# Attention with a band, then an ELU layer: tiles 8 to 17 made in pairs with 512-column products, their second products deferred

## The chip, the cores and the metric

One core of one Trainium2 chip (trn2). TensorE (PE) multiplies matrices into the eight PSUM banks; VectorE (DVE) and ScalarE (ACT) work elementwise and empty the banks; GpSimd (POOL) and SyncE (SP) mostly issue transfers. The metric is device time in microseconds of one execution, median of several runs. The profile is of one execution, and its times count from the first instruction.

## The reference, cut to what matters

```python
# q, k, v: (8, 8, 576, 64) f32
mask = abs(pos[:, None] - pos[None, :]) <= 32
scores = where(mask, q @ k.T / 8, -1e9)
attn = exp(scores - max(scores)); attn /= sum(attn)
x = (attn @ v) -> (4608, 512)        # heads side by side
h = x @ w_in                          # (4608, 2048)
g = where(h > 0, h, exp(min(h, 0)) - 1)
out = g @ w_out                       # (4608, 512), f32
```

## The kernel before

**Tiles and steps.** The 4608 rows are 18 tiles of 256 rows (NT). A tile goes through 8 steps; a step makes 2 of the 16 blocks of 128 columns of h ("first products", `products`, L716): per block four matmuls of 256 columns over the four parts of x (`xT`, 128 rows each) into one half of a PSUM bank. There are 144 steps, numbered kk, in the list `order` (L684): tiles 0 and 1 interleaved, then one tile after the other. The banks h0 and h1 take turns, so step kk needs the bank of step kk-2.

**The elementwise part.** After a step's products ScalarE makes the exponential `e_sb` (L738) and VectorE subtracts one, `m_sb` (L750; on ScalarE at L748 in steps 1, 3 and 4). One step later VectorE makes `g_sb` (L761): min of m_sb and max(h, 0), which is ELU and reads the bank a last time.

**Second products.** `mm2` (L793) multiplies the g of step kk-2 (LAG = 2) with w_out: four matmuls of 512 columns (L773), two for each half of the tile, summed in the banks y0 and y1 over the tile's 8 steps. At the tile's last step ScalarE evicts one bank, VectorE the other (`y_sb`, L290 and L292) and SyncE stores both (L811). For the last tile the second half is summed as two pieces of 256 columns (L830 to L840).

**Attention** works on pairs of blocks of 64 queries: 36 pairs, two for each tile. `begin` (L617) is the step at which a pair's work starts; from pair 10 on, both pairs of tile t begin at step 8t - 14, with exceptions in the dictionary. At begin + 0 come both pairs' scores (L384, weights from kT), at + 1 and + 2 the masks `pm` on VectorE (L404), at + 2 the products with V (L416), at + 3 and + 4 the normalisations (`rc` L425, `x_st` L428, VectorE) and a DMA transpose of x_st into xT, issued on SyncE (L455). The exponentials `pu` are on ScalarE (L395).

**Inputs.** For each of the 8 batches SyncE loads q and k in four DMAs of 576 KB (L132), ScalarE (early on also VectorE) casts them in six parts (L290, L292), ScalarE writes the rows to DRAM (L319) and SyncE reads them back transposed into qT and kT (L324). The steps of loads (l_qk), V loads (l_v) and casts (from c0) are a table by batch (L642). V comes in through GpSimd's queue (L151) into `V_e`; a copy shifted by 64 rows, `V_o`, is made by four VectorE copies (L175), or for batches 2 and 3 by two DMAs on SyncE (L183).

**Order.** The schedule is by hand: `at(kk, slot, fn)` puts work into slots of step kk, and the loop at L814 issues, for each step: g of the step before, slot "dve", the first products, slot "mid", the second products, slot "end". Each engine and each DMA queue takes its instructions in this order.

Of the kernel before, what the change touches and what calls it, by code (L numbers as in the profile page):

```python
# [21 lines left out]
def kernel(  # L22
# [99 lines left out]

    def load_qk(b, which, part, engs=(nc.sync, nc.sync)):
        z, nj = part
        mj = max(nj, HJ)
        t = lpool.tile([128, 2, mj * D], FP32, tag=f"f{which}{mj}",
                       name=f"f{which}", bufs=2 if part is WHOLE else 1)
        qk_f[b, which, z] = t
        src = (q, k)[which][b, :, z:z + NC * nj, :].rearrange(
            "(g h) (c j) d -> c g h (j d)", h=2, j=nj)  # L130
        for h in range(2):
            engs[h].dma_start(out=t[:, h, 0:nj * D], in_=src[:, :, h, :])  # L132
# [161 lines left out]
    def cast_qk(b, which, part, j0, n, eng, hs=slice(0, 2)):  # L294
        z, nj = part
        if (b, which, z) not in qk_b:
            qk_b[b, which, z] = lpool.tile(
                [128, max(nj, HJ), 2 * D], BF16,
                tag=f"b{which}{max(nj, HJ)}", name="qkb",
                bufs=2 if part is WHOLE else 1)  # L300
        t = qk_b[b, which, z]
        copy_on(eng,
                t[:, j0:j0 + n, :].rearrange("p j (h d) -> p h j d",
                                             h=2)[:, hs],
                qk_f[b, which, z][:, hs, j0 * D:(j0 + n) * D].rearrange(
                    "p h (j d) -> p h j d", d=D))
# [134 lines left out]

    xT = {}

    def xT_of(i):
        t, z = i // 2, i % 2
        if z == 0:
            xT[t] = xpool.tile([128, 2, NDO, 128], BF16, tag="xT", name="xT")
        return xT[t][:, z, :, :]

    def x_evac(i, eng=nc.vector):  # L450
# [113 lines left out]
    def at(kk, slot, fn, *args):  # L564
        tasks.setdefault((kk, slot), []).append((fn, args))
# [48 lines left out]


    FIRST_TWO, FIRST_DMA, BACK_AT = 6, 10, 18
    begin = {4: 9, 5: 12, 6: 18, 8: 26, 10: 31, 12: 37}  # L617
    for i in range(FIRST_TWO, NPAIR):
        begin[i] = begin.get(i - i % 2, STEPS * (i // 2) - 14)
    for i in range(4, NPAIR):  # L620
        two = i >= FIRST_TWO
        kk, z = begin[i], i % 2 if two else 0
# [15 lines left out]
    for b in range(2, B):  # L638
        k0 = begin[first_pair(b)]


        l_qk, l_v, c0 = {2: (0, 0, 0), 3: (15, 24, 22), 4: (35, 36, 41),  # L642
                         5: (52, 52, 57), 6: (68, 68, 73),
                         7: (84, 84, 89)}[b]
        if b >= 3:
            at(l_qk, "end", load_qk, b, 0, WHOLE)
            at(l_qk, "end", load_qk, b, 1, WHOLE)
# [1 line left out]
                at(l_v, "dve", hold_v, b)  # L649
            for m in range(VS):  # L650
                at(l_v + m, "mid", load_v, b, m)
        if b <= 3:

            if b == 2:
                at(k0, "dve", rotate_v, b, 0, 1)
            at((21, 28)[b - 2], "mid", rotate_v_dma, b, 3 - b)
        else:
            for n, back in enumerate((10, 8, 3, 2)):
                m0 = 2 * (n // 2)
                at(k0 - back, "dve", rotate_v, b, m0, m0 + 2, (n % 2,))  # L660
# [12 lines left out]
        for n, (which, j0) in enumerate(  # L673
# [3 lines left out]
            if j0 == 12:  # L677
# [3 lines left out]

    order = [(z, n + m) for n in range(0, HALF, 2) for z in range(2)  # L684
             for m in range(2)]
    order += [(z, n) for n in range(HALF, STEPS) for z in range(2)]
    order += [(t, n) for t in range(2, NT) for n in range(STEPS)]
    psH, e_t, m_t, g_t, psY = {}, {}, {}, {}, {}

    def mm1(kk):  # L690
        t, s = order[kk]
        if kk == BY_PAIRS[1]:
            return
        ks = BY_PAIRS if kk == BY_PAIRS[0] else (kk,)
        tags = ((f"h{kk % 2}", "s") if kk == NSTEP - 1 else
                ("s",) if kk == 2 else ("u",) if kk == 3 else (f"h{kk % 2}",))
        for k in ks:
            psH[k] = []
        for z, tag in enumerate(tags):
            for k in ks:  # L700
                psH[k].append(ps_tile([128, FG // len(tags), TT], FP32,
                                      tag if k == kk else "u", "ps"))
        for p in range(len(ks)):
            for k in ks:
                for z in range(len(tags)):
                    products(k, z, p if len(ks) > 1 else None)
                if p == len(ks) - 1:
                    for z in range(len(tags)):
                        exponents(k, z)
                        if k == NSTEP - 1:  # L710
                            elu(k, z)


    BY_PAIRS = (2, 3)
# [1 line left out]
    def products(kk, z, pair):  # L716
        t, s = order[kk]
        ps = psH[kk][z]
        w = ps.shape[1]
        for j in range(w):  # L720
            fo = s * FG + z * w + j
            for do in range(NDO):
# [11 lines left out]
    def exponents(kk, z):  # L734
# [5 lines left out]
        if kk > 0:  # L740
            subtract(kk, z)

    def subtract(kk, z):
        e_sb = e_t.pop((kk, z))
        m_sb = mpool.tile([128, e_sb.shape[1], TT], BF16, tag="m_sb",
                          name="m_sb")
        if kk in (1, 3, 4):
            nc.scalar.activation(m_sb, e_sb, AX.Copy, bias=-1.0)  # L748
        else:
            nc.vector.tensor_scalar(m_sb, e_sb, -1.0, None, ALU.add)  # L750
        m_t[kk, z] = m_sb

    def elu(kk, z=0):
        if z == 0:
            g_t[kk] = mpool.tile([128, FG, TT], BF16, tag="g_sb", name="g_sb",
                                   bufs=6)
        if kk == 0:
            subtract(kk, z)
        ps = psH[kk][z]
# [4 lines left out]

    out_t = out.rearrange("(t ts p) c -> t p ts c", p=128, ts=TT // 128)

    def sums_to(kk, ts, j, c):
        t, s = order[kk]
        to, cs = psY[t][ts], slice(0, D_MODEL)
        if c is not None:  # L770
            cs = slice(c * D_MODEL // 2, (c + 1) * D_MODEL // 2)
            to = psY[t][ts + c][:, 0:D_MODEL // 2]
        nc.tensor.matmul(  # L773
            to,
            lhsT=g_t[kk][:, j, ts * 128:(ts + 1) * 128],
            rhs=w_out_sb[:, s * FG + j, cs],
            start=(s == 0 and j == 0),
            stop=(s == STEPS - 1 and j == FG - 1))

    def rows_out(ts, c, eng):  # L780
        t = NT - 1
        if c is None:
            src, cs = psY[t][ts], slice(0, D_MODEL)
        else:
            cs = slice(c * D_MODEL // 2, (c + 1) * D_MODEL // 2)
            src = psY[t][ts + c][:, 0:D_MODEL // 2]
        y_sb = opool.tile([128, D_MODEL], FP32,
                          tag=f"y_sb{int(eng is nc.vector)}", name="y_sb")
        copy_on(eng, y_sb[:, cs], src)
        (nc.scalar if c == 1 else nc.sync).dma_start(  # L790
            out_t[t, :, ts, cs], y_sb[:, cs])

    def mm2(kk, parts=((0, 0), (0, 1), (1, 0), (1, 1))):  # L793
        t, s = order[kk]
        if s == 0:
            psY[t] = [ps_tile([128, D_MODEL], FP32, g, "psY")
                      for g in (("h2", "t0") if t == 1 else ("y0", "y1"))]
            if t == NT - 1:
                psY[t].append(ps_tile([128, D_MODEL], FP32, "u", "psY"))
        last = t == NT - 1  # L800
        for ts, j in parts:

            for c in ((0, 1) if last and ts else (None,)):
                sums_to(kk, ts, j, c)
        if s == STEPS - 1 and not last:
            for ts in range(2):
                eng = (nc.scalar, nc.vector)[ts]
                y_sb = opool.tile([128, D_MODEL], FP32, tag=f"y_sb{ts}",
                                  name="y_sb")
                copy_on(eng, y_sb, psY[t][ts])  # L810
                nc.sync.dma_start(out_t[t, :, ts, :], y_sb)  # L811

    LAG = 2
    for kk in range(NSTEP + LAG):  # L814
        run(kk, "first")
        for n in {1: (), 2: (0, 1)}.get(kk, (kk - 1,) if kk < NSTEP else ()):
            if n >= 0:
                elu(n)
        run(kk, "dve")
        if kk < NSTEP:  # L820
            mm1(kk)
        run(kk, "mid")

        for n in {2: (), 3: (), 4: (), 5: (0, 1), 6: (2, 3), 7: (4,), 8: (5, 6)}.get(
                kk, (kk - LAG,) if kk >= LAG else ()):

            if n < NSTEP - 2:
                run(kk, n)
                mm2(n)
            elif n == NSTEP - 1:  # L830
                for part in ((n - 1, 0, 0, None), (n - 1, 0, 1, None),
                             (n - 1, 1, 0, 0), (n - 1, 1, 0, 1),
                             (n, 0, 0, None), (n, 0, 1, None)):
                    sums_to(*part)
                rows_out(0, None, nc.scalar)
                for c in range(2):
                    for part in ((n - 1, 1, 1, c), (n, 1, 0, c),
                                 (n, 1, 1, c)):
                        sums_to(*part)
                    rows_out(1, c, (nc.vector, nc.scalar)[c])  # L840
        run(kk, "end")


# [28 lines left out]
```

## Time and profile before

| | us |
|---|---|
| median of 3 runs | 303.45 (303.1 to 303.76) |
| the profiled execution, its own time | 303.12 |
| its span, first to last instruction | 301.4 |
| PE busy | 294.1 |
| DVE busy | 240.9 |
| ACT busy | 170.1 |
| POOL busy | 50.3 |
| L728, first products, x1168 | 149.2 |
| L773, second products, x592 | 147.5 |
| L761, g_sb, x145 | 99.3 |
| L750, m_sb, x142 | 61.5 |

Busy times of one engine may overlap: a matmul's end is modelled and reaches into the next one, so PE's rows add up to more than they take; the distances between starts tell the pace. A row of a timeline has start, length, engine, line, operation, what it writes and reads, and how many were merged; a bracket at its end is the engine's idle time before it and what ended that.

### The profile page before, as it was taken

The numbers are of one execution on the slowest core, as the hardware profiler recorded it, in microseconds if no ns is written. First come the engines' busy times: TensorE is split into PE (matmuls) and PEld (weight loads), VectorE is DVE, ScalarE is ACT, GpSimd is POOL, SyncE is SP. The second block draws the span as 40 slices with busy tenths as digits, with TensorE's granted clock in tenths as the row PEclk, the third lists the DMA queues.
The fourth block names the chain that finished last, engine by engine and source line by source line (L and its number), as shares of the span: only waits on it lengthen the run. The fifth ranks groups of instructions, "written<-read, shape, count | busy, mean of one in ns | idle before, by whom it ended". The sixth has DMA issues, their size and how long they took to land.

```text
span 301.4 us, 7717 instructions
## 1 busy us (share of the span) xinstructions
PE 294.1 (98%) x3118; PEld 198.4 (66%) x3118; DVE 240.9 (80%) x479; ACT 170.1 (56%) x258; POOL 50.3 (17%) x72
## 2 busy tenths in 40 slices
PE   7999999999999999999999999999999999999994
PEld 3675667677666666666666666666666666666673
DVE  6778587988787988888888888877888787877663
ACT  3783558688655567456745674466535353533332
POOL 8857103620005000410032003200000000000000
PEclk9999999999999999999999999999999999999999
DMA  9999999999967948999899979997921111111012
GB/s 190 183 200 206 187 238 366 362 147 219 254 156 191 250 111 265 234 274 143 161 258 331 157 206 256 306 148 148 270 40 72 35 72 38 70 37 70 2 70 71
DMA packets 93157, 52.68 MB, mean 175 GB/s; under 512 B 77122, under 2 KB 83010, under 8 KB 93122
## 3 DMA queue, kind: packets, MB, share of 16 engines
q1 hardware_dynamic: 47330, 35.48, 44.3%
q0 software_dynamic: 43920, 10.10, 44.2%
q10 hardware_dynamic: 1872, 6.62, 6.4%
q8 instruction: 24, 0.39, 0.6%
q14 instruction: 11, 0.09, 0.1%
HBM read 36.70 MB, written 15.34 MB: 173 GB/s over the span
## 4 chain that ended last, share of the span: by engine, by line
PE 93%; DVE 2%; ACT 1%; DMA 1%; issue 1%; DVEq 0%; ACTq 0%
PE ps L728 42%; PE psY L773 41%; PE psS L416 4%; PE psS L384 3%; DMA f<-in_q_dram 1%; PE ptx L340 1%; PE psXT L438 1%; ACT pu L395 1%; PE ptx L335 1%; DVE qkb L292 1%; PE psS L364 1%; DVE x_st L428 0%; ACT qT L290 0%; PE ps_idle L479 0%; DVE pm L404 0%
## 5 line engine op out<-in xcount | busy, mean ns | idle before, releaser
L738 ACT ACTIVATE e_sb<-ps 128x512 f32<-128x512 f32 (+1 forms) x145 | 86.2, 595 | 114.9 <-PE ps L728 106.9
L728 PE MATMUL ps<-xT,w_in_sb 128*128 128x256 bf16 (+1 forms) x1168 | 149.2, 271 | 0.0
L773 PE MATMUL psY<-w_out_sb,g_sb 128*128 128x512 bf16 (+1 forms) x592 | 147.5, 374 | 0.0
L728 PEld LDWEIGHTS <-w_in_sb 128*128 128x128 bf16 x1168 | 110.8, 98 | 36.3 <-issue 0.5
L761 DVE SCALAR_TENSOR_TENSOR g_sb<-ps,m_sb 128x512 bf16<-128x512 f32 (+1 forms) x145 | 99.3, 686 | 13.1 <-DVE m_sb L750 0.5
L750 DVE TENSOR_SCALAR m_sb<-e_sb 128x512 bf16<-128x512 f32 (+1 forms) x142 | 61.5, 433 | 34.4 <-ACT e_sb L738 32.4
L773 PEld LDWEIGHTS <-g_sb 128*128 128x128 bf16 x592 | 56.1, 98 | 38.5 <-DVE g_sb L761 0.3
L151 POOL DMA_DIRECT2D Ve<-in_v_dram x37 | 31.7, 868 | 133.5 <-PE psS L416 79.9
L395 ACT ACTIVATE pu<-psS 128x1024 bf16<-128x1024 f32 x36 | 36.5, 1021 | 1.3 <-PE psS L384 1.3
L428 DVE TENSOR_TENSOR x_st<-psS,rc 128x512 bf16<-128x512 f32 x36 | 24.9, 691 | 1.2
L290 ACT CAST qkb<-f 128x768 bf16<-128x768 f32 (+1 forms) x29 | 25.0, 861 | 0.0
L404 DVE TENSOR_TENSOR pm<-pu,masks 128x1024 bf16<-128x1024 bf16 x32 | 21.8, 682 | 0.4 <-ACT pu L395 0.4
L416 PEld LDWEIGHTS <-pm 128*64 128x64 bf16 x512 | 9.7, 110 | 7.4 <-DVE pm L404 6.1
L292 DVE COPY y_sb<-psY 128x512 f32<-128x512 f32 (+1 forms) x18 | 12.1, 670 | 1.1 <-PE psY L773 1.1
L384 PEld LDWEIGHTS <-kT 64*128 64x128 bf16 x560 | 9.3, 95 | 4.4 <-issue 4.0
L290 ACT COPY y_sb<-psY 128x512 f32<-128x512 f32 (+1 forms) x19 | 10.9, 572 | 1.7 <-PE psY L773 1.7
L416 PE MATMUL psS<-Ve,pm 128*64 128x65 bf16 x288 | 11.6, 196 | 0.1
L384 PE MATMUL psS<-qT,kT 64*128 64x64 bf16 x560 | 11.5, 191 | 0.1
L416 PE MATMUL psS<-Vo,pm 128*64 128x65 bf16 x224 | 10.3, 196 | 0.0
L175 DVE COPY Vo<-Ve 64x1040 bf16<-64x1040 bf16 (+1 forms) x22 | 9.1, 414 | 0.7
L290 ACT COPY qT<-ptx 128x1152 bf16<-128x1152 bf16 (+4 forms) x9 | 7.7, 881 | 3.4 <-PE ptx L340 2.5
L425 DVE RECIPROCAL rc<-psS 128x8 f32<-128x8 f32 x36 | 7.2, 199 | 0.9 <-PE psS L416 0.9
(54 smaller groups left out, 88.2 us busy)
## 6 DMA issues: line engine op xcount, KB each, us to landing
out_dram<-y_sb SPq DMA_DIRECT2D x35, 256.0 KB, 3.3
f<-in_q_dram SPq DMA_DIRECT2D x12, 576.0 KB, 6.3
f<-in_k_dram SPq DMA_DIRECT2D x12, 576.0 KB, 8.3
in_dram<-qkb ACTq DMA_DIRECT2D x10, 576.0 KB, 4.3
Ve<-in_v_dram POOLq DMA_DIRECT2D x21, 128.0 KB, 12.6
w_in_sb<-in_moe_w_in_dram POOLq DMA_DIRECT2D x3, 512.0 KB, 10.1
w_out_sb<-in_moe_w_out_dram POOLq DMA_DIRECT2D x3, 512.0 KB, 10.9
Ve<-in_v_dram POOLq DMA_DIRECT2D x14, 96.0 KB, 11.5
```

The source lines that it names most:

```text
L151: nc.gpsimd.dma_start(out=V_e[b % 3][p0:p1, m, :, 0:D], in_=v[b, :, lo + p0:lo + p1, :].rearrange("h p d -> p h d"))
L290: nc.scalar.copy(d_, s_)
L384: nc.tensor.matmul(psS[:, h % 2, hp * 128 + z * QB:hp * 128 + (z + 1) * QB], lhsT=keys, rhs=qT[b % 2][base:base + 64, hp, QB * qb:QB * (qb ...
L395: nc.scalar.activation(pu, _bap(psS, [psS.ap[0], [1, 1024]]), AX.Exp, scale=SCALE)
L404: nc.vector.tensor_mul(pm, pu, _bap(mm, [mm.ap[0], [0, H], [1, 2 * QB]]))
L416: nc.tensor.matmul(psS[QB * z:QB * (z + 1), par, hp * VD:(hp + 1) * VD], lhsT=pm[:, par * HP + hp, z * QB:(z + 1) * QB], rhs=vv[:, qb // 2 ...
L428: nc.vector.tensor_mul(x_st, _bap(psS, [psS.ap[0], [VD, HP], [512, 2], [1, D]]), _bap(rc, [rc.ap[0], [2, HP], [1, 2], [0, D]]))
L728: nc.tensor.matmul(o, lhsT=w_in_sb[:, do, fo * 128:(fo + 1) * 128], rhs=r, start=(do == 0), stop=(do == NDO - 1))
L738: nc.scalar.activation(e_sb, ps, AX.Exp)
L750: nc.vector.tensor_scalar(m_sb, e_sb, -1.0, None, ALU.add)
L761: nc.vector.scalar_tensor_tensor(g_t[kk][:, z * w:(z + 1) * w, :], ps, 0.0, m_t.pop((kk, z)), ALU.max, ALU.min)
L773: nc.tensor.matmul(to, lhsT=g_t[kk][:, j, ts * 128:(ts + 1) * 128], rhs=w_out_sb[:, s * FG + j, cs], start=(s == 0 and j == 0), stop=(s == ...
```

## The change

- From tile 8 on (WIDE) two tiles share a step: one block of h for 512 rows, four matmuls of 512 columns instead of eight of 256. The xT of two tiles is one buffer; the operand is four runs of 128 columns. Steps, exponentials, m_sb and g_sb keep their number and size.
- Second products of tiles 2 to 16 come from a list `todo`, in the old order, up to four in a step; in "light" steps (begin + 0, 5, 6, from pair 16 on also 7) three, until 48 are behind. By the code's counting 12 are behind at step 18, 36 at step 64, 48 from step 87 on. An eviction follows its tile's last sum, and no further sum is issued in that step. g_sb gets 23 buffers instead of 6.
- The last tile's second products all come after everything else, as pieces of 512, 384 and 128 columns; VectorE evicts the last two, and ScalarE's queue stores the last.
- Attention begins earlier: at 8t - 18 instead of 8t - 14 from tile 10 on (tiles 7, 8 and 9 at 42, 47, 53 instead of 42, 50, 58), and loads, V loads and casts of batches 4 to 7 with it by 4 or 5 steps.
- At begin + 4 of tiles 5 to 9 the subtraction is on ScalarE. V_o of batch 4 is made by DMA instead of by VectorE.
- The load and cast buffers of half and whole batches share two slots.

```diff
-        mj = max(nj, HJ)
-        t = lpool.tile([128, 2, mj * D], FP32, tag=f"f{which}{mj}",
-                       name=f"f{which}", bufs=2 if part is WHOLE else 1)
+        t = lpool.tile([128, 2, SJ * D], FP32, tag=f"f{which}",
+                       name=f"f{which}")
...
+    WIDE = 8
     def xT_of(i):
-        t, z = i // 2, i % 2
+        n = 2 if i < 2 * WIDE else 4
+        t, z = i // n * n // 2, i % n
         if z == 0:
-            xT[t] = xpool.tile([128, 2, NDO, 128], BF16, tag="xT", name="xT")
+            xT[t] = xpool.tile([128, n, NDO, 128], BF16, tag=f"xT{n}",
+                               name="xT", bufs=4 if n == 2 else 2)
...
-    begin = {4: 9, 5: 12, 6: 18, 8: 26, 10: 31, 12: 37}
+    begin = {4: 9, 5: 12, 6: 18, 8: 26, 10: 31, 12: 37, 14: 42, 16: 47, 18: 53}
     for i in range(FIRST_TWO, NPAIR):
-        begin[i] = begin.get(i - i % 2, STEPS * (i // 2) - 14)
+        begin[i] = begin.get(i - i % 2, STEPS * (i // 2) - 18)
...
-        l_qk, l_v, c0 = {2: (0, 0, 0), 3: (15, 24, 22), 4: (35, 36, 41),
-                         5: (52, 52, 57), 6: (68, 68, 73),
-                         7: (84, 84, 89)}[b]
+        l_qk, l_v, c0 = {2: (0, 0, 0), 3: (15, 24, 22), 4: (30, 31, 36),
+                         5: (48, 48, 53), 6: (64, 64, 69),
+                         7: (80, 80, 85)}[b]
...
-        if b <= 3:
+        if b <= 4:
...
-            at((21, 28)[b - 2], "mid", rotate_v_dma, b, 3 - b)
+            at((21, 28, 40)[b - 2], "mid", rotate_v_dma, b, int(b == 2))
...
-    order += [(t, n) for t in range(2, NT) for n in range(STEPS)]
+    order += [(t, n) for t in range(2, WIDE) for n in range(STEPS)]
+    made = {(t, n * FG + j): (kk, j * TT)
+            for kk, (t, n) in enumerate(order) for j in range(FG)}
+    for t in range(WIDE, NT, 2):
+        for fo in range(NFO):
+            for z in range(2):
+                made[t + z, fo] = len(order), z * TT
+            order.append((t, fo))
...
+        if t >= WIDE:
+            for do in range(NDO):
+                nc.tensor.matmul(
+                    _bap(ps, [ps.ap[0], [128, 4], [1, 128]]),
+                    lhsT=w_in_sb[:, do, s * 128:(s + 1) * 128],
+                    rhs=xT[t][:, :, do, :],
+                    start=(do == 0), stop=(do == NDO - 1))
+            return
...
+    on_scalar = {1, 3, 4} | {begin[2 * t] + 4 for t in range(5, 10)}
...
-                                   bufs=6)
+                                   bufs=23)
...
+    todo = [(t, n * FG + j, ts) for t in range(2, NT - 1)
+            for n in range(STEPS) for ts in range(2) for j in range(FG)]
+    light = {begin[i] + n for i in range(FIRST_TWO, NPAIR)
+             for n in ((0, 5, 6) if i < 16 else (0, 5, 6, 7))}
+    LEAD = 10 * 2 * FG
+    def more_sums(kk):
+        behind = (kk + 1 - STEPS * 2) * 2 * FG - (576 - 64 - 32 - len(todo))
+        n = 3 if kk in light and behind < LEAD + 8 else 4
+        while todo and n:
+            t, fo, ts = todo[0]
+            if made[t, fo][0] > kk - LAG:
+                break
+            todo.pop(0)
+            if fo == 0 and ts == 0:
+                begin_sums(t)
+            sums_to(t, fo, ts)
+            n -= 1
+            if fo == NFO - 1 and ts == 1:
+                for ts in range(2):
+                    rows_out(t, ts)
+                break
+    def last_sums():
+        t = NT - 1
+        begin_sums(t)
+        for ts, c, eng, queue in ((0, 0, nc.scalar, nc.sync),
+                                  (1, 1, nc.vector, nc.sync),
+                                  (1, 2, nc.vector, nc.scalar)):
+            for fo in range(NFO):
+                sums_to(t, fo, ts, c)
+            rows_out(t, ts, c, eng, queue)
...
-    for kk in range(NSTEP + LAG):
+    kk = 0
+    while kk <= NSTEP or todo:
...
+        if kk >= 2 * STEPS + LAG:
+            more_sums(kk)
...
+        kk += 1
+    last_sums()
```

## The prediction

> **What bounds the kernel now.** I read the busy table of the page, then the chain of work that ended last, then the timelines of TensorE, VectorE and SyncE in a stretch with attention.
>
> ```profile
> PE 294.1 (98%) x3118; PEld 198.4 (66%) x3118; DVE 240.9 (80%) x479; ACT 170.1 (56%) x258; POOL 50.3 (17%) x72
> ...
> PE 93%; DVE 2%; ACT 1%; DMA 1%; issue 1%; DVEq 0%; ACTq 0%
> ```
>
> TensorE is busy nearly throughout and carries 93% of the chain. A busy PE may still be a slow one, so the starts decide (timeline of PE; start, length, count):
>
> ```profile
> 218.35 1.04 PE L728 MATMUL ps<-xT,w_in_sb 128*128 128x256 bf16 x8
> 219.23 1.03 PE L773 MATMUL psY<-w_out_sb,g_sb 128*128 128x512 bf16 x4
> 220.09 1.04 PE L728 MATMUL ps<-xT,w_in_sb 128*128 128x256 bf16 x8
> 220.96 1.03 PE L773 MATMUL psY<-w_out_sb,g_sb 128*128 128x512 bf16 x4
> ```
>
> Step 102 starts at 218.35, step 103 at 220.09: 1.737 us. Eight first products take 0.873 (109 ns each, start to start), four second products 0.864 (216 each), with nothing between: the matrix engine is at its pace. From 20 us on all starts together exceed that pace by about 9 us, some 8 of them at the changes of shape round the attention's small products. Under 1 us is waiting, so no wait worth removing is left; what remains to gain is instruction count and the end.
>
> How near is the next limit? The bank that a step's products fill is free when VectorE has made the g_sb of two steps before (timeline of DVE, same stretch):
>
> ```profile
> 218.85 0.69 DVE L761 SCALAR_TENSOR_TENSOR g_sb<-ps,m_sb 128x512 bf16<-128x512 f32 x1
> 219.46 0.20 DVE L425 RECIPROCAL rc<-psS 128x8 f32<-128x8 f32 x1
> 219.69 0.69 DVE L428 TENSOR_TENSOR x_st<-psS,rc 128x512 bf16<-128x512 f32 x1
> 220.30 0.42 DVE L750 TENSOR_SCALAR m_sb<-e_sb 128x512 bf16<-128x512 f32 x1
> 220.82 0.69 DVE L761 SCALAR_TENSOR_TENSOR g_sb<-ps,m_sb 128x512 bf16<-128x512 f32 x1
> ```
>
> The last row is the g_sb of step 102. It ends at 221.51, and step 104, which needs its bank, starts at 221.83: 0.32 spare, of which 0.05 is the signal (at 206.50 PE started 0.054 after the g_sb that it had waited for). Where nothing queues on VectorE the spare is 0.55 (step 103, for one); after a normalisation, as here, 0.32.
>
> **The change part by part.**
>
> *Half as many first products in tiles 8 to 17.* 640 products of 256 columns become 320 of 512, on the path throughout. Two of the old take 218 ns and one of 512 columns takes 216 in the rows above: 320 x 2.2 ns = 0.7 us gained. The weight loads that go (98 ns each) lay under the products. VectorE's and ScalarE's counts per step stay.
>
> The Trainium skill (TensorE: Matmul & The Clock Gate, Back-to-back issue gap) gives 131 ns for a sustained product of 512 columns; by that this part would gain 320 x 87 ns = 28 us. The rows have 216 for the same product, so the measurement decides.
>
> *The end.* Now the last product ends at 297.60, the last store lands at 300.45, the span closes 0.93 later. Afterwards the last piece is 128 columns on VectorE (684 ns for 512 and 425 for 256 make some 295) instead of 256 on ScalarE (372), and the 256 KB and 192 KB pieces leave earlier: 0.06 + 0.30 + 0.03 + 2.25 (the 128 KB store's landing) = 2.64 after the product instead of 2.85. I take 0.2 gained (0 to 0.45). The products of the last tile cost the same in sum (16 x 216, 16 x 162, 16 x 56).
>
> *The backlog.* Paired tiles need all 16 blocks before the first of the two can be summed, so the second products must be deferred: in "light" steps three are issued, not four, until 48 lie behind (step 87). PE's total is unchanged; each light step is 216 ns shorter while VectorE's and ScalarE's work in it stays. Two light steps in a row eat 0.43 of the 0.55 spare: no wait by themselves. With anything else on VectorE there is one, and everything on PE behind it waits too. Counting forward from the starts above: the V rotations (0.43 each, at steps 67, 68, 76, 83, 84, all light) cost 0.19, 0.20, 0.14, 0.20, 0.20; step 81 evicts a tile and step 82 normalises, ahead of light step 83: 0.39. Together 1.3 us. In steps 18 to 63 the same sum gives 0.2 at step 25 (a cast of 0.85 us behind two light steps), 0.3 at 37 and 0.2 at 60 to 62; there five subtractions go to ScalarE, so I take 0.4 of this 0.7.
>
> *The eviction of psY moves.* Before, it came at step 105, beside a long attention step. The order of the built program now has it at steps 90, 98, 106, 114 and 122, just where the normalisation delays VectorE, between subtraction and g_sb. Its price, from the place where it stands now:
>
> ```profile
> 225.26 0.43 DVE L750 TENSOR_SCALAR m_sb<-e_sb 128x512 bf16<-128x512 f32 x1 [0.33 <-ACT e_sb L738]
> 225.61 0.68 DVE L292 COPY y_sb<-psY 128x512 f32<-128x512 f32 x1
> 226.21 0.68 DVE L761 SCALAR_TENSOR_TENSOR g_sb<-ps,m_sb 128x512 bf16<-128x512 f32 x1
> ```
>
> Subtraction to g_sb is 0.95 instead of 0.52: 0.43 later. Against 0.32 - 0.05 of spare, and 0.02 that the shorter steps take: 0.19 of waiting, five times: 0.9 us. The chain of VectorE thus gives 1.3 + 0.4 + 0.9 = 2.6 us (0 if every spare is larger than I read, 3.5 with the early 0.7 and casts of ScalarE in the way).
>
> *Loads pulled forward on SyncE.* Attention starts four steps earlier, and q/k loads with it. In two places this turns the queue's order round: the four loads of batch 4 (issued at step 30) now stand ahead of the k transpose of batch 3 (step 32), those of batch 5 (48) ahead of that of batch 4 (49). Before, the transpose went first (SyncE's timeline):
>
> ```profile
> 121.01 2.72 SPq L324 DMA_TRANSPOSE kT<-in_dram  x1
> 123.77 1.24 SPq L132 DMA_DIRECT2D f<-in_q_dram  x2
> 125.05 1.60 SPq L132 DMA_DIRECT2D f<-in_k_dram  x2
> 126.71 3.17 SPq L455 DMA_TRANSPOSE xT<-x_st  x2
> ```
>
> The transposes of xT behind these loads show what that place costs; the summary of xT has
>
> ```profile
> DMA to landing us min/median/max: 2.4/2.7/9.7
> ```
>
> and the two here landed after 9.0 and 8.6, after the last load (134.06, 10.3 after the first was issued). The k transpose (0.59 MB, about 3.5 us of transfer, 5.8 from issue to landing alone) would land some 13.8 after the first load's issue. Batch 3: the loads can start at 79.5, as soon as SyncE is through with the q transpose, so kT is there at 93.3; the scores that need it come at 92.0 (before: 93.9; nine deferred products earlier): 1.3 late at most, nothing if the transpose does not queue; I take 0.5. Batch 4: loads 5.0 after the start of step 45, kT at +18.8, its scores at +15.5 (eight steps, now 14.7, and one set of products): 3.3 late at most, 0 at least; the xT rows are the nearest, but they had V loads beside them from the start, so I take 1.9. Behind the waiting weight load stands all of PE.
>
> The Trainium skill (DMA: Bandwidth & Descriptors, Queues, rings and completion order) says that SyncE's transfers share one row of rings, taken in order on each DMA engine, which speaks against this order; by it both waits would come whole, 4.6 us, and without it none. The skill's page TensorE: Matmul & The Clock Gate (Part 1: The HAM clock gate) puts the engine to half clock after some 3.4 us without work, which such a wait comes near; no row here shows it, the granted clock being 9 tenths or more in every slice.
>
> *Off the path.* Four V copies (0.43 each) of batch 4 leave VectorE for two DMAs on SyncE, under attention's lead; shared load buffers are reused only after casts of two batches back, long done. If one were not, SyncE would stop at the load, and its later transposes with it.
>
> **Sum** on the profiled execution (303.12, 301.4 of it span): -0.7 - 0.2 + 2.6 + 2.4 = +4.1, so 307.2; the median of the runs shown is 0.33 higher: **307.5**.
>
> **The rivals.**
> - *The transposes come in time* (0.21). For it: before, k landed 4 to 8 us ahead of its scores in the later batches. Against: the 9.0 us rows. VectorE's waits stay: 303.45 - 0.9 + 2.6 = 305.2 (304 to 306).
> - *The spare holds* (0.25, the other side). Before, PE waited under 1 us in 280 with VectorE at 80%; if the five subtractions on ScalarE and the long steps between the light ones absorb the eviction and rotations, and k lands early, only the gain is left: 302.5 (302 to 302.8). It decides as soon as all waits together stay under 0.3 us; at 0.9 nothing is left.
> - *Gain and waits cancel* (0.10): waits of 0.3 to 1.5 us, 302.85 to 304.05.
> - *Worse than forecast* (0.05): every wait at its upper end, -0.9 + 3.5 + 4.6 = +7.2, 310.6.
> - The forecast itself, both kinds of waiting: 0.39, 305.6 to 309.8.
>
> A measurement of this kernel tells some 0.2% (0.6 us) from no change: faster 0.25, same 0.10, slower 0.65. The range of 8 in 10 runs from 302.3, inside the clean case, to 309.8.
>
> **What would show it.** Products of 512 columns starting every 216 ns; half as many weight loads for the first products of tiles 8 to 17; PE waiting for g_sb by 0.2 at steps 92, 100, 108, 116, 124 and by 0.1 to 0.4 in 67 to 86; weight loads of the scores idle on the transposes of kT at steps 37 and 53, by 0.5 and 2 us. I am wrong if PE shows no wait there, or if a product that reads four runs of 128 columns streams slower than 216 ns (each 10 ns more is 3.2 us).

## The result, and the profile after

The changed kernel takes 327.07 us (median of 6 runs, 325.02 to 329.94), the kernel before, run beside it, 303.55 (303.1 to 303.78): ratio 1.076, 95% interval 1.071 to 1.081. Here and below a ratio leaves out slow runs, those more than 1.5% above the fastest of their kernel (one of these six, two of four in e7_v_later). The prediction said 307.5 with a range of 302.3 to 309.8: the direction was right, the time lies 17 us above the range. The profiled execution took 327.38, its span is 325.5, 24.1 more than before.

The page of the changed kernel (span; busy time by engine; granted clock by slice; the chain that ended last, by engine):

```profile
span 325.5 us, 7073 instructions
...
PE 301.8 (93%) x2798; PEld 168.8 (52%) x2798; DVE 237.1 (73%) x469; ACT 172.9 (53%) x261; POOL 50.0 (15%) x72
...
PEclk9999999999995999859999999999999999999999
...
PE 65%; DMA 15%; DVE 8%; ACT 4%; issue 3%; SPq 2%; POOL 1%; ACTq 0%; DVEq 0%; POOLq 0%
```

TensorE's share of the chain fell from 93% to 65%, and DMA, 1% before, now carries 15% (the chain follows a late transfer back to its issue, so this share is larger than the time waited). Two slices show a granted clock of half; before, none did. VectorE is less busy than before and is not the new bound. The view of waits names the transfer (engine, line, releaser: us in total, times, longest):

```profile
PEld L381 <- DMA kT<-in_dram: 14.0, 2, 7.5
PE psS L381 <- DMA kT<-in_dram: 13.6, 2, 7.4
...
PE psY L798 <- ACT y_sb L289: 1.4, 2, 0.9
```

Two waits of the scores for the k transpose make 13.6 us. TensorE's timeline round the first (start, length, operation, count, idle before and releaser):

```profile
93.62 0.52 PE L381 MATMUL psS<-qT,kT 64*128 64x64 bf16 x24
101.54 0.40 PE L381 MATMUL psS<-qT,kT 64*128 64x64 bf16 x8 [7.39 <-DMA kT<-in_dram]
...
103.12 1.92 PE L745 MATMUL ps<-xT,w_in_sb 128*128 128x256 bf16 x8
```

24 of the 32 score products use what is there; the other 8 wait 7.39 us for the k transpose of batch 3. Then, at 103.12, eight first products take 1.92 us; with the clock full they take 1.04 in this view. The table by stretches (engine, us busy and instructions, then granted clock, DMA share, GB/s) shows why:

```profile
101.70:105.00 3.30, 3.30 (x20) 1.86 (x17) 0.00 (x0) 0.00 (x0) 0.00 (x0) 0.50 1.17 267
105.00:115.00 10.00, 10.00 (x125) 6.73 (x123) 7.21 (x14) 7.50 (x11) 0.00 (x0) 1.00 0.33 94
...
140.70:146.00 5.30, 5.30 (x28) 2.83 (x23) 3.03 (x6) 2.90 (x4) 0.00 (x0) 0.50 0.47 128
```

After each of the two waits TensorE runs on at a granted clock of 0.50, until 105.06 and until 146.02. Step 38 took 2.69 us instead of the 1.74 of a step of its kind, and the whole costs about 4.5 us (half of the 3.30 and of the 5.30 in these stretches, and some 0.3 in the scores just ahead of the second). SyncE's timeline shows the transfer itself:

```profile
79.64 1.67 SPq L131 DMA_DIRECT2D f<-in_q_dram  x2
81.35 1.30 SPq L131 DMA_DIRECT2D f<-in_k_dram  x2
87.16 7.72 SPq L321 DMA_TRANSPOSE kT<-in_dram  x1
94.97 1.22 SPq L457 DMA_TRANSPOSE xT<-x_st  x1
```

The k transpose was issued at 87.16, and issuing it alone held SyncE for 7.72 us (2.72 in the line shown of before). It landed at 101.49, 14.3 after its issue; the one of batch 4, issued at 126.18, landed at 139.84, 13.7 after. In the kernel before the same two took 5.8 and 5.4. The summary of the k transposes, before and after, and what GpSimd's queue moved beside the first one (V, from 84 to 102 us: packets, MB, share of the 16 DMA engines):

```profile
DMA to landing us min/median/max: 4.6/5.8/6.8
```

```profile
DMA to landing us min/median/max: 4.0/7.1/14.3
```

```profile
q0 software_dynamic: 4688, 0.59, 58.1%
```

The shared products are as fast as forecast (TensorE's timeline, steps 100 and 101):

```profile
231.68 1.04 PE L731 MATMUL ps<-xT,w_in_sb 128*128 128x512 bf16 x4
232.55 1.03 PE L798 MATMUL psY<-w_out_sb,g_sb 128*128 128x512 bf16 x4
233.41 1.03 PE L731 MATMUL ps<-xT,w_in_sb 128*128 128x512 bf16 x4
```

233.41 - 231.68 = 1.73 for a dense step (1.727 over many) against 1.737: 0.8 us gained over 80 steps. The eviction stands where the forecast put it (VectorE's timeline, steps 98 and 99):

```profile
230.01 0.41 DVE L769 TENSOR_SCALAR m_sb<-e_sb 128x512 bf16<-128x512 f32 x1
230.34 0.68 DVE L291 COPY y_sb<-psY 128x512 f32<-128x512 f32 x1
230.94 0.68 DVE L780 SCALAR_TENSOR_TENSOR g_sb<-ps,m_sb 128x512 bf16<-128x512 f32 x1
```

g_sb ends at 231.62, and the products that need its bank start at 231.68, 0.16 later than the four sums before them allow (230.65 + 0.87 = 231.52).

**Where 24.1 us went**: 13.6 two waits for k; 4.5 half clock after them; 5.5 smaller waits (0.8 five evictions, 1.6 light steps and rotations, 1.7 first sums waiting for ScalarE's eviction, 1.4 exponentials behind casts); less 0.8 shared products and 0.5 the end. The remaining 1.8 is spread in pieces under 0.25, half of it in the first 20 us; I did not trace it.

### The profile page after: what moved, and what is told of

It reads as the page before. It is cut to its first block, busy times and chain, and to the rows that moved or that the text cites. A ratio compares the mean times of both kernels' runs of the same rounds, so it can differ in the third digit from the quotient of the medians.

```text
span 325.5 us, 7073 instructions
## 1 busy us (share of the span) xinstructions
PE 301.8 (93%) x2798; PEld 168.8 (52%) x2798; DVE 237.1 (73%) x469; ACT 172.9 (53%) x261; POOL 50.0 (15%) x72
## 4 chain that ended last, share of the span: by engine, by line
PE 65%; DMA 15%; DVE 8%; ACT 4%; issue 3%; SPq 2%; POOL 1%; ACTq 0%; DVEq 0%; POOLq 0%
PE psY L798 29%; PE ps L731 17%; PE ps L745 11%; DMA kT<-in_dram 9%; DVE g_sb L780 3%; PE psS L413 2%; DMA f<-in_q_dram 2%; PE psS L381 2%; DVE m_sb L769 2%; DMA in_dram<-qkb 2%; DMA c<-in_q_dram 2%; ACT e_sb L755 2%; DVE pm L401 1%; DVE x_st L425 1%; PE ptx L337 1%
## 5 line engine op out<-in xcount | busy, mean ns | idle before, releaser
L798 PE MATMUL psY<-w_out_sb,g_sb 128*128 128x512 bf16 (+2 forms) x592 | 149.5, 377 | 1.4 <-ACT y_sb L289 1.4
L755 ACT ACTIVATE e_sb<-ps 128x512 f32<-128x512 f32 x144 | 86.0, 598 | 120.5 <-PE ps L731 66.1
L780 DVE SCALAR_TENSOR_TENSOR g_sb<-ps,m_sb 128x512 bf16<-128x512 f32 x144 | 99.1, 689 | 13.7 <-ACT m_sb L767 1.9
L769 DVE TENSOR_SCALAR m_sb<-e_sb 128x512 bf16<-128x512 f32 x136 | 58.9, 433 | 47.9 <-ACT e_sb L755 46.1
L731 PE MATMUL ps<-xT,w_in_sb 128*128 128x512 bf16 x320 | 82.2, 379 | 0.8 <-DVE g_sb L780 0.7
L745 PE MATMUL ps<-xT,w_in_sb 128*128 128x256 bf16 (+1 forms) x528 | 68.4, 275 | 0.7 <-DVE g_sb L780 0.7
L745 PEld LDWEIGHTS <-w_in_sb 128*128 128x128 bf16 x528 | 50.0, 100 | 17.3 <-issue 3.1
L731 PEld LDWEIGHTS <-w_in_sb 128*128 128x128 bf16 x320 | 30.1, 98 | 39.6 <-DVE g_sb L780 3.2
L381 PE MATMUL psS<-qT,kT 64*128 64x64 bf16 x560 | 12.2, 194 | 13.7 <-DMA kT<-in_dram 13.6
L291 DVE COPY y_sb<-psY 128x512 f32<-128x512 f32 (+2 forms) x19 | 12.5, 656 | 15.2 <-PE psY L798 15.2
L289 ACT COPY y_sb<-psY 128x512 f32<-128x512 f32 x18 | 10.5, 582 | 5.7 <-PE psY L798 5.7
```

Of the source, the lines that this page charges most:

```text
L289: nc.scalar.copy(d_, s_)
L381: nc.tensor.matmul(psS[:, h % 2, hp * 128 + z * QB:hp * 128 + (z + 1) * QB], lhsT=keys, rhs=qT[b % 2][base:base + 64, hp, QB * qb:QB * (qb ...
L731: nc.tensor.matmul(_bap(ps, [ps.ap[0], [128, 4], [1, 128]]), lhsT=w_in_sb[:, do, s * 128:(s + 1) * 128], rhs=xT[t][:, :, do, :], start=(do ...
L745: nc.tensor.matmul(o, lhsT=w_in_sb[:, do, fo * 128:(fo + 1) * 128], rhs=r, start=(do == 0), stop=(do == NDO - 1))
L755: nc.scalar.activation(e_sb, ps, AX.Exp)
L780: nc.vector.scalar_tensor_tensor(g_t[kk][:, z * w:(z + 1) * w, :], ps, 0.0, m_t.pop((kk, z)), ALU.max, ALU.min)
```

## The experiments

Theory A, after the result: the transposes are late because four loads stand ahead of them in SyncE's queue, and every other loss is small. That V packets have a part in it came in only with e3. Rivals: attention four steps earlier asks more of the DMA engines than they give, in whatever order, the longer lag of the second products, or VectorE's chain. "k 3" below is the k transpose of batch 3.

**1. Loads behind the transposes** (e1_loads_behind), and only those of batch 5 (e2_one_behind):

```diff
-        4: (30, 31, 36), 5: (48, 48, 53)
+        4: (32, 31, 38), 5: (50, 48, 53)      # e1
+        4: (30, 31, 36), 5: (49, 48, 53)      # e2
```

> The changed kernel with the loads of batch 4 and 5 put behind the k transposes of batch 3 and 4 again (steps 32 and 50 instead of 30 and 48; the casts of batch 4 two steps later, so that they need not wait for the loads). Theory A (a k transpose queued behind four loads is late, and the idle matrix engine then runs at half clock for a while): the two waits of 7.4 and 6.2 us at the scores go, and with them 4.5 us of half clock, so 327.1 - 18.1 = 309 (308 to 311), k landing some 6 us after its transpose is issued. Rival B (attention four steps earlier asks more of the DMA engines than they give, in whatever order): k stays late by several us at both places, 320 or more.

Measured: 319.34, ratio 1.048 (1.042 to 1.054). The waits for k shrink to 0.8 and 1.5, though k 3 and k 4 still took 10.2 and 9.1 us from issue to landing instead of the expected 6, with no load ahead of them and V packets beside them. In place of these waits TensorE waits for the x of tile 5, whose transpose now stands behind the loads (issued 89.86, landed 102.29), and half clock follows for 3.41 us:

```profile
105.36 1.86 PE L745 MATMUL ps<-xT,w_in_sb 128*128 128x256 bf16 x8 [5.56 <-DMA xT<-x_st]
```

So a transpose of x is late in that place too, with V packets beside it as well. The time lies at the edge of the rival's range, not at A's 309, because the wait changed its victim.

> The changed kernel with only the loads of batch 5 behind the k transpose of batch 4 (step 49 instead of 48). A: only the second wait goes (6.2 us, and 2.9 us of half clock after it): about 318; the first, of 7.4 us, stays as it was. B: nothing moves by more than 2 us.

Measured: 316.42, ratio 1.039 (1.030 to 1.048). As expected, the second wait is gone (k 4 issued 121.97, landed 126.58), the first stays with 5.3, and half clock lasts 6.83 us once. One number of the table moves 10.7 us. The first wait was 7.4 in the changed kernel although nothing ahead of it was edited, so such a wait can differ by 2 us between two executions.

**2. The order turned in the kernel before** (e3_before_flipped):

```diff
-        4: (35, 36, 41), 5: (52, 52, 57)
+        4: (30, 36, 41), 5: (51, 52, 57)
```

> The kernel before with nothing changed but this order: loads of batch 4 at step 30 instead of 35, of batch 5 at 51 instead of 52, so that they stand ahead of the k transposes of batches 3 and 4. A: k of batch 3 lands near 101 us as in the changed kernel, its scores are wanted at 93.7: about 7 us of wait and 2 of half clock, and 0 to 2 us at batch 4: 311 to 314. B: 303.5 to 304.5, since nothing starts earlier as a whole. The rule of my prediction (the transpose takes its own 3.5 us after the loads have landed): 304 to 305.

Measured: 310.35, ratio 1.017 (1.008 to 1.026): nothing else of the change is in this kernel, and two numbers cost 6.6 us. But the two places differ. k 3, behind four loads, landed 7.0 after its issue and in time. k 4, behind the loads and beside V packets, took 14.4:

```profile
133.90 1.04 PE L728 MATMUL ps<-xT,w_in_sb 128*128 128x256 bf16 x8
138.88 1.03 PE L384 MATMUL psS<-qT,kT 64*128 64x64 bf16 x32 [3.94 <-DMA kT<-in_dram]
139.84 1.89 PE L773 MATMUL psY<-w_out_sb,g_sb 128*128 128x512 bf16 x4
```

The place behind the loads alone is thus not enough; the V packets matter.

**3. Work put into the waits** (e4_filled_wait): 30 and 26 products with zeros, whose results are overwritten, ahead of the scores of pairs 13 and 18.

```diff
+        for n in range({13: 30, 18: 26}.get(i, 0)):
+            nc.tensor.matmul(psS[:, n % 2, :], lhsT=zeros[:, 0:128], rhs=zeros, start=True, stop=True)
```

> The changed kernel with 30 and 26 products of zeros issued just before the scores that wait (pairs 13 and 18); their sums are overwritten by the scores. They fill the two waits with work that no one needs. A: the waits end when they did (101.5 and 139.9 us in the trace), but the granted clock stays whole, so the 4.5 us of half clock after them go: 322.5 (321.5 to 324). If the slow products after the waits come from something else than the idle time, 327 or more.

Measured: 327.76, ratio 1.073 (1.064 to 1.082), no gain in time. The half clock after the first wait is gone (clock 1.00 in the stretch that had 0.50, and step 38 back at 1.74), which shows that the idle wait makes it:

```profile
101.70:105.00 3.30, 3.22 (x29) 2.20 (x30) 0.47 (x2) 1.20 (x2) 0.00 (x0) 1.00 1.13 316
```

But k 4 landed at 139.94, as in the changed kernel (139.84): the time saved ahead of it is only waited longer. What the shorter half clock after the second wait saved went into later waits (1.68 instead of 0.48 at step 71, for one). The expected 322.5 fell: with a transfer as the bound, TensorE's clock ahead of it is not on the path.

**4. V loads later** (e7_v_later) and **loads on GpSimd's queue** (e8_other_queue), each in the changed kernel:

```diff
-        4: (30, 31, 36)                                # e7: V loads at 36, V_o at 46
+        4: (30, 36, 36)
...
+        q2 = (nc.gpsimd if b in (4, 5) else nc.sync,) * 2     # e8
+        at(l_qk, "end", load_qk, b, 0, WHOLE, q2)
+        at(l_qk, "end", load_qk, b, 1, WHOLE, q2)
```

> The changed kernel with the V loads of batch 4 at step 36, as before, instead of 31 (and the V_o transfer that needs them at 46 instead of 40). In the kernel before with the flipped order k of batch 3 landed at 94.4, and 7 us later in the changed one. If GpSimd's V packets beside the loads make that difference, k lands near 95 here and the first wait falls from 7.4 to 1 to 2 us, without half clock: 318 to 321. If not, 326 or more.

Measured: 327.72 (323.63 to 329.68), ratio 1.070 (1.065 to 1.074); the profiled run took 323.63. Where the V loads were moved away, k 3 landed 8.0 after its issue instead of 14.3, and its wait fell from 7.4 to 1.0. Everything then came earlier at batch 4, where loads and V packets still meet: k 4 took 15.4, and TensorE waited 10.0. The total missed the expectation; the place where the edit was made did what it said.

> The changed kernel with the q and k loads of batches 4 and 5 issued from GpSimd's queue instead of SyncE's, at the same steps; bytes and order of the work stay. Theory A (the place behind the loads in one queue): the k transposes are issued in 2 to 4 us and land 6 to 8 after, the waits of 7.4 and 6.2 and the 4.5 of half clock go: 308 to 311. Rival B (the bytes, in whatever queue): 320 or more, the transposes being late just the same.

Measured: 319.8, ratio 1.054 (1.048 to 1.059). The loads of batch 4 are off SyncE's queue. The edit did more than that: GpSimd, whose queue runs ahead, issued them from 66.4, 13 us sooner than SyncE had, and they had landed by 85.6, before k 3 was even issued. Yet (SyncE's timeline, then TensorE's):

```profile
79.99 7.74 SPq L321 DMA_TRANSPOSE qT<-in_dram  x1
87.92 8.78 SPq L321 DMA_TRANSPOSE kT<-in_dram  x1
```

```profile
101.36 0.39 PE L381 MATMUL psS<-qT,kT 64*128 64x64 bf16 x8 [8.01 <-DMA kT<-in_dram]
```

k 3 took 13.4 from issue to landing with only V packets beside it (issued on POOL from 83.5, the last landed at 100.9) and the q transpose right ahead. My theory of a place in one queue falls here. At batch 4 the transpose went ahead of the loads and took 5.7.

**5. V packets alone** (e9_v_beside), in the kernel before:

```diff
-        5: (52, 52, 57)
+        5: (52, 47, 57)
```

> The kernel before with one issue moved: the V loads of batch 5 are issued at step 47 instead of 52, so that GpSimd's small packets move beside the k transpose of batch 4, with none of the four q and k loads in flight. In the kernel before that transpose took 5.4 us from its issue (121.0) to its landing (126.4), alone; the scores want it at about 134. Theory A (small V packets alone make a transpose slow): it lands 8 to 12 us after its issue. Theory B (only loads and packets together make it slow): 5 to 6.5 us. Theory C (only a place behind loads in SyncE's queue counts): 5.4 us. Time under all three 303.5 to 304.5, since the scores do not want it sooner.

Measured: 303.71 against 303.71, ratio 1.000 (0.999 to 1.001). The packets ran from 116 to 129, earlier than I had meant: k 4 met only their tail and took 6.5. But the q transpose of the same batch stood beside them. The summary of transposes of q into qT, in the kernel before and in this one:

```profile
DMA to landing us min/median/max: 4.4/6.1/6.3
```

```profile
DMA to landing us min/median/max: 5.8/6.1/10.0
```

The 4.4 and the 10.0 are the same transfer (batch 4, issued 115.12 and 115.44), with no q or k load in flight; ScalarE's write of k's rows runs beside it in both. So V packets with no load ahead more than double it; the kernel before pays nothing, because its scores come 8 us later. Taken together, from issue to landing:

| transpose, kernel | beside it | us |
|---|---|---|
| k 4, before; k 4, e2 | no load ahead, hardly a V packet | 5.4; 4.6 |
| k 3, e3; k 3, e7 | q and k loads ahead | 7.0; 8.0 |
| q 4, e9 | V packets | 10.0 (4.4 in before) |
| k 3, k 4, e1 | V packets, loads behind | 10.2, 9.1 |
| k 3, e8 | V packets, q transpose ahead | 13.4 |
| k 3, k 4, after; k 4, e3; k 4, e7 | loads and V packets | 14.3, 13.7; 14.4; 15.4 |
| k 3, e2; k 3, k 4, e4 | loads and V packets | 14.5; 16.4, 14.2 |

The bytes of V alone do not make the difference: in the kernel before, ScalarE's queue moved 0.59 MB in 144 packets beside the q transpose of batch 5, which took 6.1; in e9 it was 0.48 MB in 3,796 packets of V, and 10.0. Whether it is the number of packets or GpSimd's queue, no run here separates.

The Trainium skill (DMA: Bandwidth & Descriptors, Issuing engines are not separate DMA queues) says that transfers of all issuing engines run on the same 16 DMA engines and interleave there; e8 and e9 agree, and add the size: 13.4 and 10.0.

**6. Attention two steps later, loads and V behind both transposes** (e5_two_steps), then with the light steps moved to begin + 0, 2, 3 (e5_light_moved):

```diff
-    begin = {... 14: 42, 16: 47, 18: 53};  8t - 18
-        4: (30, 31, 36), 5: (48, 48, 53), 6: (64, 64, 69), 7: (80, 80, 85);  V_o by DMA for b <= 4
+    begin = {... 14: 42, 16: 49, 18: 56};  8t - 16
+        4: (35, 36, 40), 5: (51, 51, 55), 6: (66, 66, 71), 7: (82, 82, 87);  V_o by DMA for b <= 3
...
-             for n in ((0, 5, 6) if i < 16 else (0, 5, 6, 7))}
+             for n in (0, 2, 3)}                # e5_light_moved only
```

> The changed kernel with attention only two steps earlier than before (8t - 16; tiles 7, 8, 9 at 42, 49, 56), loads of batches 4 to 7 at 35, 51, 66, 82 with casts from 40, 55, 71, 87, V_o of batch 4 on VectorE as before: every k transpose, and the xT transposes of tile 5, stand ahead of the next loads again. Pairs of tiles, backlog and light steps stay. Theory A2 (the last run moved the wait from kT to xT: whichever transpose stands behind four loads is some 10 us late, and four steps of lead leave no place where none does): no transfer is waited for; left are the gain of 0.9 and VectorE's and ScalarE's waits in and after light steps, some 4: 306 to 307.5. Rival C (pairs of tiles cost much by themselves, by the four-run operand or the 23 g_sb): 310 or more.

Measured: 308.76, ratio 1.018 (1.014 to 1.021): 18.3 us less than the changed kernel. No wait for k, no half clock in the span, and no wait left after 168 us. By the sum above the waits for k and the half clock were 18.1, so the transfers account for it, though evictions moved too; 5 us above the kernel before stay.

> As the run with attention two steps earlier, and the light steps at begin + 0, 2, 3 (which attention makes long on the matrix engine) instead of begin + 0, 5, 6 and 7. If waits of VectorE's chain come from light steps in a row beside rotations, as the prediction counts them, they go, apart from some 0.5 to 1.0 us at evictions: 303 to 304.3. If the light steps do not matter: the same as the run before it.

Measured: 308.29, ratio 1.016 (1.012 to 1.020), not told apart from the one above. The waits in light steps went, and others came: 1.97 at 130.7, where ScalarE stood in a cast for a q load that landed at 130.2, 0.58 at 163 for the same reason, 0.5 to 0.7 for evictions.

**7. The rest** (e10_tuned: as the last, casts of batches 5 to 7 three steps later, a tile's last sums ahead of the middle of the step, and, which its expectation does not name, the five subtractions back on VectorE; e11_narrow: the same without shared products; e12_attention_earlier: the kernel before with attention, loads and casts of e10 alone):

```diff
+        5: (51, 51, 58), 6: (67, 67, 74), 7: (83, 83, 90)     # e10, e11, e12
+    WIDE = 18                                                 # e11
+    begin = {... 14: 42, 16: 49, 18: 56};  8t - 16            # e12, in the kernel before
```

> The kernel after with attention begun two steps earlier in a tile (8t-16), q, k and V loads behind the two transposes, light steps at 0, 2 and 3, as in the run with lights moved (308.3), and two things more: the casts of batches 5 to 7 three steps later, so that ScalarE does not stand for a q load that is still on its way (waits of 2.0 and 0.6 us there), and the last second products of a tile issued ahead of the step's middle, so that their eviction is not waited for (0.5 and 0.7 us). Theory A (the change loses only through the waits that its new order makes): 303 to 305. Theory B (a loss lies in the shared products or the longer lag themselves): still 307 or more.

> The same as the tuned kernel beside it, but no two tiles share their first products: 256 columns each, from tile 8 on too. It isolates what sharing is worth. By the rows (80 dense steps of 1.727 us instead of 1.737) sharing gains 0.8 us, and two tiles in one step cost the longer chains on VectorE in light steps; narrow products are expected 0.5 to 1.5 us slower than the tuned kernel if the shared products gain what the rows say, and equal or faster if the chains of paired tiles eat it.

> The kernel before with attention alone begun two steps earlier (8t-16, tiles 7 to 9 at 42, 49 and 56) and loads and casts as in the tuned kernel; no shared first products, second products two steps behind as before, no step with fewer of them. With the tuned kernel (308.8) and its narrow twin (309.5) it makes a ladder. Theory A (the tuned kernel loses through the steps with fewer second products and the evictions that these move): this one stays at 303.5 to 305.0. Theory B (the earlier attention itself makes the waits, through casts, loads and masks that meet on ScalarE and VectorE): 307 or more. In between the loss is shared in proportion.

Measured: 308.80 (ratio 1.017, 1.015 to 1.019), 309.48 (1.020, 1.018 to 1.021), 309.53 (1.019, 1.016 to 1.021). The medians alone would misread all three; the distance between the scores of two successive tiles, in the steady part, sorts them. TensorE's timeline of e10, e11 and e12:

```profile
222.04 0.64 PE L381 MATMUL psS<-qT,kT 64*128 64x64 bf16 x32
...
237.28 0.64 PE L381 MATMUL psS<-qT,kT 64*128 64x64 bf16 x32
```

```profile
222.42 0.64 PE L381 MATMUL psS<-qT,kT 64*128 64x64 bf16 x32
...
237.73 0.64 PE L381 MATMUL psS<-qT,kT 64*128 64x64 bf16 x32
```

```profile
211.88 0.64 PE L384 MATMUL psS<-qT,kT 64*128 64x64 bf16 x32
...
227.70 0.64 PE L384 MATMUL psS<-qT,kT 64*128 64x64 bf16 x32
```

15.24 per tile with shared products, 15.31 without, 15.82 in e12; the kernel before has 15.32 and the changed kernel 15.41 (with its eviction beside the normalisation). Sharing is worth 0.08 per tile, 0.8 in ten tiles (0.7 between the medians of e10 and e11, as expected), and e10 is the faster once it runs steadily; the whole of its 5 us is lost between 80 and 190 us, in a dozen waits of 0.2 to 1.3 while the backlog is built. The longest, at 171.37, is VectorE standing for a buffer that an xT transpose behind the loads still reads:

```profile
169.49 0.69 DVE L425 TENSOR_TENSOR x_st<-psS,rc 128x512 bf16<-128x512 f32 x1 [1.39 <-DMA xT<-x_st]
```

By its number e10 sides with theory B of its expectation, by its trace with A: my repairs moved waits rather than removing them. In e12 the 0.50 per tile (nine tiles, 4.5 of its 6 us) is none of the things that I had named. The eviction has come to stand behind the attention's exponential on ScalarE (its timeline, then TensorE's):

```profile
214.90 1.02 ACT L395 ACTIVATE pu<-psS 128x1024 bf16<-128x1024 f32 x1
215.80 0.59 ACT L290 COPY y_sb<-psY 128x512 f32<-128x512 f32 x1
```

```profile
215.06 1.04 PE L728 MATMUL ps<-xT,w_in_sb 128*128 128x256 bf16 x8
216.44 1.02 PE L773 MATMUL psY<-w_out_sb,g_sb 128*128 128x512 bf16 x4 [0.34 <-ACT y_sb L290]
```

The first products take 0.87 from start to start, so the first sum of the next tile could start at 215.94 and waits 0.50 for its bank. It is the same kind of wait as the 1.0 at step 64 of the changed kernel, where ScalarE also did the exponential ahead of the eviction. Since e12 has neither the backlog nor sharing, its nearness to e11 is no proof that attention's place costs e11 its 6 us; that part stays open.

No version beat the kernel before. The most that the change can give, by these rows, is 0.8 for sharing and 0.5 to 0.9 at the end (from the last product to the end of the span 3.30 in the changed kernel, 2.89 in e10, 3.78 before), some 302; a schedule that reaches it would need the backlog built without a single wait, and I have not found one.

## Why the prediction was wrong, point by point

- **Half as many first products**: right. 216 ns for 512 columns in four runs of 128, 0.8 gained for a forecast 0.7.
- **The end**: right in kind; from the last product to the end of the span 3.30 instead of 3.78, 0.5 for 0.2. Of this the last store landed 2.0 after the last product (2.64 forecast), while the close took 1.29 instead of 0.93.
- **The backlog**: right. Waits of 0.17, 0.20, 0.15, 0.54, 0.20, 0.20 at steps 68, 69, 75 to 77, 83, 84, 85, for 0.19, 0.20, 0.14, 0.39, 0.20, 0.20.
- **The eviction of psY moves**: right for VectorE, five waits of 0.16 to 0.17 for 0.19. What I left out is ScalarE's half of it: where a tile's last step has one or two sums, the next tile's first sum comes at once and waits for y0 (0.7 and 1.0 at steps 36 and 64). Also missed: exponentials come late behind casts on ScalarE, at step 59 behind a subtraction, a cast and the issue of a write (0.9), at step 71 behind a cast that stands for a q load (0.5). Together 3.1 us in steps that I had priced at 0.4.
- **Loads pulled forward on SyncE**: this step failed, by its size. It said "The k transpose (0.59 MB, about 3.5 us of transfer, 5.8 from issue to landing alone) would land some 13.8 after the first load's issue", and took 0.5 and 1.9 us of waiting, 4.6 at most; it was 7.4 and 6.2, and with the half clock 18.1 us for 2.4. The start was right: the first loads went at 79.64 (79.5 forecast) and had landed 11.1 later (10.3). The need was right for batch 4, 15.5 after the start of step 45 (15.5), and 2.1 later than forecast for batch 3 (94.1 for 92.0), which by itself would have removed that wait. The landing was not: 21.9 and 16.3 after the first load's issue, that is 10.7 and 6.1 after the last load had landed, where I had added 3.5. I priced the transpose as one that has the DMA engines to itself once the loads are through. But the change moves the V loads forward as well (step 36 to 31 and 52 to 48), and GpSimd's packets, 4,682 of a batch's 4,688 for k 3 and 4,035 for k 4, then run beside the transpose, which e9 shows to be enough without the loads (4.4 to 10.0). For k 4 the time of the V loads hardly moved (125.7 for 124.7); there the transpose, issued at 126.2 instead of 121.0, came to stand among them. I had read of V loads only that they spoiled the xT rows as a model, and lowered my price for it; they were the reason to raise it. In e3, with no other part of the change, the pair costs 6.6 us.
- **Half clock**: named in the prediction from the Trainium skill and priced at nothing. The rows now show it: 0.50 for 6.83 and 10.24 us, 4.5 us of cost.
- **The rivals**: even "worse than forecast" (310.6) kept my bound of 4.6 for the two transposes, so no case, and no end of the range, allowed a transfer twice as long.

## What to carry to other kernels

When an issue is moved on one queue, list what the other queues will have in flight at that moment: beside the packets of another queue a transpose took 10 us instead of 4.4 here, and its time alone is no upper bound. A bound on a wait must come from the slowest row of the same kind of transfer, with its neighbours counted, not from a time alone plus a place in a queue. When a schedule is shifted by some steps, look for what each eviction now stands behind on its own engine, and compare the distance between repeats in the steady part before believing a total.

## What the runs showed of the hardware

- The half clock came in multiples of 3.41 us: 3.41 (e1, after an idle wait of 5.6; e4, 2.1), 6.83 (e2, 5.3; e3, 3.9; the changed kernel, 7.4), 10.24 (e7, 10.0; e8, 8.0; the changed kernel, 6.2). The Trainium skill (TensorE: Matmul & The Clock Gate, Part 1: The HAM clock gate) gives a free-running window of 3413 ns, which these lengths agree with; how long an idle time led to how many windows was not the same from case to case.
- Issuing a k transpose held SyncE for 2.3 to 2.7 us in the kernel before, for 7.7 and 7.5 in the changed one (loads ahead) and 8.8 in e8 (the q transpose ahead), and the transposes of x wait behind it in the queue. In e1, with no load ahead, it was 2.7 and 2.2, though the landing took 10.2 and 9.1.
- Work that keeps the clock up in a wait (e4) gains nothing as long as a later transfer lands at the same time: 139.94 and 139.84.
